# Keys, queries and values of the first image as single products, and integer additions of 512 in two-engine turns

## The chip, the cores and the metric

The kernel runs on one core of a Trainium2 chip. The metric is device time in microseconds for one execution; the time before is the median of three runs. Engines: TensorE (PE), VectorE (DVE), ScalarE (ACT), GpSimd (POOL) and SyncE (SP), which issues the DMAs.

## The reference, cut to what matters

Four images of 8 heads with 576 tokens of 64 numbers. Attention has two branches which are added: one over means of four neighbouring tokens (144), repeated four times; one over tokens nearer than four. Its output is x, 2304 rows of 512. Two layers of 512 to 2048 to 512 follow, each with a gate and with float64 weights.

```
q_d = q.reshape(B, H, Sd, 4, D).mean(axis=3)   # k_d, v_d the same
out = repeat(sm_attn(q_d, k_d, v_d), 4) + local_attn(q, k, v)   # |i - j| < 4
h = x @ w_in;  g = h * (1 / (1 + exp(-h)));  x = g @ w_out
h = x @ w2_in; g = h * (1 / (1 + exp(-1.702 * h))); out = g @ w2_out
```

## The kernel before

**Stages.** Attention goes by half images m (0 to 7) of 288 tokens; within one, by four pairs of heads. One pair of one half is a unit u = 4 m + pair (0 to 31). A finished half is scaled and split into two f16 parts (`split`: maximum over all, `rm`, `am`, `pw`; the parts `xh`, `xl`) and runs through layer 1 as 288 columns (`h1.m.p`, line 706, then `o1`, lines 823 and 851), three products per weight tile. Layer 2 takes the rows in nine tiles of 256 (`h2`, line 885; `o2`, line 964). The maximum of a layer 2 tile is spread over partitions by a diagonal (`dx`, lines 766 and 768) and a product of 128 columns (`rm`, line 775).

**Image 0 (units 0 to 7).** k and q arrive with tokens in partitions. `KT` (lines 1132 and 1134) turns k by six transposes of 96 columns and sums four tokens at a time by six f32 products of 24 columns against `four`; `KC` copies both out on ACT. `QT` (1177, 1179) and `QC` do it for q with three and three. From image 1 on DVE turns and sums instead (`KX`, `KD`, `QX`, `QD`). v is loaded twice: `vw` in windows for the local branch and `vraw` (`lv`) for the sums over four tokens, which POOL adds (`KV`, lines 1153 and 1154).

**A unit.** `SC` scores (1203, 1209), `DM`, `LC`, `LS`, `LE`, `LU`, `RC` and `LN` the two softmaxes, `DE` the exponentials of the first branch, `DN` its scaling (line 1256 on ACT, 1258 on DVE), `TP`/`TC` and `PT` turn the probabilities, `AV` (1285, 1291) multiplies by v, `UC` and `XA` add the branches, `XM` takes the maximum. `KT` uses one two-bank tile; `QT`, `TP`, `AV` and `rm` share a ring of two one-bank PSUM tiles, `pa1`.

**First weights.** Each 1 MB piece of float64 words becomes f32 integers by `ca`, `cz` (ACT), `cs` (DVE, line 332), `sg` (the sign: ACT line 345, or DVE line 337) and `cp`, an addition of 1024 integers per partition (line 349; on DVE or POOL). PE sums the upper halves (`sps`, lines 561 and 576) for a scale (`si`, `so`), and `hi` (ACT) and `lo` (DVE, line 381) make the f16 parts. `cp` of the second weights is an addition of 512 on POOL. There are eight pieces for `in` and eight for `out`, named by column block and row pair (0.0, 0.2, 1.0 ...).

**Order.** Every step is added to a plan with its engine, the tiles it reads and writes and the rings it takes. `ON` (line 25) puts chosen steps on an engine other than the usual one. `PLACES` (line 46) holds two characters per step: its place in one total order; `placed` sorts by it and refuses an order that breaks a dependency. Each engine, and SP's queue of DMAs, then works through its steps in that order; an instruction that waits holds all behind it. The list `first` (line 1478) chains the first loads softly.

## Time and profile before

| | |
|---|---|
| median of 3 runs | 893.99 us (892.43 to 894.34) |
| the profiled execution | 892.67 us, its span 890.9 us |
| PE busy | 864.1 us (97%), 10212 matmuls |
| PE weight loads | 721.5 us |
| DVE busy | 608.9 us, 1334 instructions |
| ACT busy | 470.4 us, 841 |
| POOL busy | 160.8 us, 187 |
| HBM read, written | 62.39 MB, 13.11 MB |

Busy time is the union of an engine's instructions, and matmuls are pipelined: a run of matmuls counts from the first start to the last end. An average over the span hides stages, so the rows below go by stretches of time. Matmuls of f32 are two instructions each; a transpose is one.

### The profile page before, as it was taken

To read this page: it belongs to the slowest core of one execution; us is meant where nothing else is said; L and a number is where in the kernel's file an instruction comes from. 1 tells how busy PE (TensorE), PEld (TensorE's weight loads), DVE (VectorE), ACT (ScalarE), POOL (GpSimd) and SP (SyncE) were. 2 spreads that over 40 slices of the span, in tenths; PEclk is the share of its full clock that TensorE was granted. 3 is DMA by queue.
4 is the path that set the end of the run, shared out by engine and by line. 5 is a ranking of instruction groups with operands and counts; after the bars stand their busy time and mean duration, and the time that the engine had idled before them with its cause. 6 is when DMAs were issued, how large, how long until landed. Compare 5 with 4: busy or idle time off the path is not lost.

```text
span 890.9 us, 23880 instructions
## 1 busy us (share of the span) xinstructions
PE 864.1 (97%) x10212; PEld 721.5 (81%) x10212; DVE 608.9 (68%) x1334; ACT 470.4 (53%) x841; POOL 160.8 (18%) x187
## 2 busy tenths in 40 slices
...
GB/s 241 228 244 226 199 100 86 45 120 67 120 114 117 88 156 140 152 80 135 116 61 248 101 43 1 25 1 24 2 13 1 25 24 1 37 1 25 1 25 24
DMA packets 116190, 77.04 MB, mean 86 GB/s; under 512 B 94836, under 2 KB 101492, under 8 KB 115060
## 3 DMA queue, kind: packets, MB, share of 16 engines
...
q14 instruction: 26, 0.21, 0.1%
HBM read 62.39 MB, written 13.11 MB: 85 GB/s over the span
## 4 chain that ended last, share of the span: by engine, by line
PE 84%; DVE 11%; ACT 2%; issue 1%; DMA 0%; SPq 0%; DVEq 0%; ACTq 0%
PE ops L823 19%; PE hps L706 18%; PE hps L885 18%; PE oy L964 10%; PE oz L964 5%; PE ox L964 3%; PE ul L1291 2%; PE sl L1209 2%; PE ops L851 2%; DVE g L913 1%; PE sl L1203 1%; PE ul L1285 1%; DVE wout L381 1%; PE tps L1268 1%; PE kps L1134 1%
## 5 line engine op out<-in xcount | busy, mean ns | idle before, releaser
L706 PE MATMUL hps<-xhl,win 128*128 128x288 f16 x1536 | 197.9, 287 | 0.1
L885 PE MATMUL hps<-xhl,win 128*128 128x256 f16 x1728 | 190.4, 273 | 1.3 <-DVE tg L900 1.3
L885 PEld LDWEIGHTS <-win 128*128 128x128 f16 x1728 | 169.1, 98 | 21.2 <-issue 1.6
L706 PEld LDWEIGHTS <-win 128*128 128x128 f16 x1536 | 148.5, 98 | 37.8 <-issue 0.4
L823 PE MATMUL ops<-g,wout 128*128 128x288 f16 x1344 | 171.7, 286 | 0.0
L964 PEld LDWEIGHTS <-g 128*128 128x128 f16 x1512 | 147.7, 98 | 18.6 <-issue 0.8
L823 PEld LDWEIGHTS <-wout 128*128 128x128 f16 x1344 | 129.5, 98 | 32.7 <-issue 0.6
L897 ACT ACTIVATE tg<-hps,blk 128x512 f32<-128x512 f32 x72 | 49.5, 687 | 123.9 <-PE hps L885 111.2
L900 DVE SCALAR_TENSOR_TENSOR tg<-tg,hps 128x512 f32<-128x512 f32 x72 | 49.1, 682 | 53.1 <-ACT tg L897 53.1
L913 DVE SCALAR_TENSOR_TENSOR g<-tg,g 128x896 f16<-128x896 f32 x72 | 78.1, 1097 | 0.6 <-ACT g L910 0.3
L904 POOL TENSOR_TENSOR tg<-tg 128x128 f32<-128x128 f32 x19 | 15.1, 793 | 341.9 <-DVE tg L900 341.9
L910 ACT ACTIVATE g<-tg 128x896 f16<-128x896 f32 x72 | 67.5, 945 | 16.1 <-DVE tg L906 12.0
L964 PE MATMUL oy<-wout,g 128*128 128x256 f16 x648 | 75.1, 272 | 0.0
L349 POOL TENSOR_TENSOR cs<-cs,cz 128x512 int32<-128x512 int32 x32 | 43.9, 1378 | 149.0 <-DVE cs L332 67.7
L718 ACT ACTIVATE tg<-hps,blk 128x576 f32<-128x576 f32 x64 | 47.0, 734 | 34.4 <-PE hps L706 27.7
L721 DVE SCALAR_TENSOR_TENSOR tg<-tg,hps 128x576 f32<-128x576 f32 x64 | 47.6, 744 | 18.8 <-ACT tg L718 18.8
L942 ACT ACTIVATE o<-oy,blk 128x256 f32<-128x256 f32 x27 | 12.7, 472 | 76.8 <-PE oy L964 76.8
L731 DVE SCALAR_TENSOR_TENSOR g<-tg,gs,g 128x576 f16<-128x576 f32 x56 | 46.4, 839 | 9.7 <-ACT g L728 9.7
L728 ACT ACTIVATE g<-tg,gs 128x576 f16<-128x576 f32 x56 | 42.7, 769 | 14.6 <-DVE tg L721 14.6
L948 DVE SCALAR_TENSOR_TENSOR o<-oy,blk,o 128x256 f32<-128x256 f32 x9 | 4.4, 484 | 55.4 <-PE oy L964 55.4
L324 ACT ACTIVATE st<-st 128x512 f32<-128x512 f32 (+1 forms) x48 | 39.5, 827 | 2.0 <-DMA st<-in_moe_w_out_dram 2.0
L1239 ACT ACTIVATE pd<-sl,nm 72x144 f32<-72x144 f32 x64 | 23.4, 369 | 16.3 <-DVE nm L1219 12.0
...
## 6 DMA issues: line engine op xcount, KB each, us to landing
...
```

What stands on the lines that cost most here:

```text
L349: eng.tensor_tensor(out=s, in0=s, in1=zget(), op=ALU.add)
L706: nc.tensor.matmul(o, T[w][:, kc, a, fc * P:(fc + 1) * P], T[xk][:, kc, b, :T_], start=(n == 0), stop=(n == 3 * KC - 1))
L718: ACT.activation(out=T[tg], in_=T[ps][:, :, :T_], func=AF.Tanh, scale=T["a" + bk][:, c:c + 1])
L721: DVE.scalar_tensor_tensor(out=T[tg], in0=T[tg], scalar=1.0, in1=T[ps][:, :, :T_], op0=ALU.add, op1=ALU.mult)
L731: DVE.scalar_tensor_tensor(out=T[g][:, 1], in0=T[tg], scalar=gs, in1=T[g][:, 0], op0=ALU.mult, op1=ALU.subtract)
L823: nc.tensor.matmul(o, w[:, j, a, dc * P:(dc + 1) * P], g[:, b, j % 2, :], start=(n == 0), stop=(n == 3 * NF - 1))
L885: nc.tensor.matmul(o, T[w][:, kc, a, fc * P:(fc + 1) * P], T[xk][:, kc, b, :], start=(n == 0), stop=(n == 3 * KC - 1))
L897: ACT.activation(out=four(), in_=T[ps][:, 0, :], func=AF.Tanh, scale=T["a" + bk][:, c:c + 1])
L900: DVE.scalar_tensor_tensor(out=four(), in0=four(), scalar=1.0, in1=T[ps][:, 0, :], op0=ALU.add, op1=ALU.mult)
L910: ACT.activation(out=T[g][:, 0], in_=T[tg], func=AF.Copy, scale=GS2)
L913: DVE.scalar_tensor_tensor(out=T[g][:, 1], in0=T[tg], scalar=GS2, in1=T[g][:, 0], op0=ALU.mult, op1=ALU.subtract)
L964: nc.tensor.matmul(T[bank[acc]], g[:, a, slot, :], w, start=first and p == p0 and i == 0, stop=prod in (2, 3, 4) and p == NF // 2 - 1 and ...
```

## The change

In image 0 the transposes and sums of k and q become one product per 128 columns of input: the moving matrix is `four` beside the identity (24 + 96 = 120 columns), so `KT` has six products and `QT` three, and `KC`, `QC` and the scores' addresses follow the new layout. `lv` and `KV` go for image 0; `VP` sums v by six products per pair of heads from `vw` against a new constant `vsum`, and `VC` copies the result out on ACT. `VP` takes a turn in `pa1`. `cap` makes the new constants. Each `cp` of the first weights is two additions of 512, `a` and `b`, placed one by one. In layer 2 the step `dx` goes, and `rm` has 4 columns. `GS2`, a power of two in layer 2's g, is changed. `ON` and `PLACES` are new: among other things the load of the first piece of weights is issued ahead of q and k, in the order weights 0.0, q0, k of pair 0, q1, k of pair 1, `vw` of pair 0, weights 1.0. On PE, `QT0` comes ahead of `KT0.0`, `QT1` ahead of `SC0`, and `VP0.0` stands between `KT0.1` and `SC1`. On POOL, three halves of `cp` stand ahead of `LS3`, and one between `LS3` and `LN3`. In all 26 halves go to POOL and 6 to DVE, of seven whole ones on POOL and nine on DVE before. Of `gs2`, 14 steps stay on POOL, of 19.

```diff
--- before.py
+++ after.py
@@ -20,18 +20,20 @@
 NEG = -1.0e9
 SCD = 1.0 / 128.0
 
-GS1, GS2 = 2.0 ** -15, 2.0 ** -26
+GS1, GS2 = 2.0 ** -15, 2.0 ** -19
 BAND = 4
 ON = {
-    "DVE": ("sg1.in.0.2 sg1.in.1.0 sg1.in.1.2 sg1.in.2.2 sg1.in.3.0 sg1.in.3.2 sg1.out.0.2 LS0 LN1 LN2 LS3 LS8 LN8 LN10 "
...
-    "POOL": ("cp1.out.0.0 cp1.out.0.2 cp1.out.1.0 cp1.out.1.2 cp1.out.2.0 cp1.out.2.2 cp1.out.3.2"),
-    "ACT": ("DN0 DN1 DN2 DN3 DN5 DN6 DN7 DN8 DN9 DN10 DN11 DN12 DN13 DN14 DN15 DN16 DN17 DN18 DN19 DN20 DN21 DN23 DN24 DN25 "
...
+    "DVE": ("sg1.in.0.0 sg1.in.1.0 sg1.in.2.2 sg1.in.3.0 sg1.out.0.0 sg1.out.1.0 LS0 LN0 LN2 LS4 LN5 LN8 LS9 LS10 LN10 LS13 "
...
+    "POOL": ("cp1.in.0.0a cp1.in.0.2b cp1.in.1.0a cp1.in.1.0b cp1.in.1.2b cp1.in.2.0a cp1.in.2.2a cp1.in.2.2b cp1.in.3.0a "
+             "cp1.in.3.0b cp1.in.3.2a cp1.in.3.2b cp1.out.0.0a cp1.out.0.0b cp1.out.0.2a cp1.out.1.0a cp1.out.1.0b "
+             "cp1.out.1.2a cp1.out.1.2b cp1.out.2.0a cp1.out.2.2a cp1.out.2.2b cp1.out.3.0a cp1.out.3.0b cp1.out.3.2a "
+             "cp1.out.3.2b"),
+    "ACT": ("DN2 DN4 DN5 DN6 DN7 DN8 DN11 DN12 DN13 DN15 DN17 DN20 DN21 DN22 DN30 DN31"),
...
@@ -344,9 +346,9 @@
             else:
                 ACT.activation(out=l1, in_=hi.bitcast(F32), func=AF.Copy)
 
-        def cp(eng):
-            s = r().bitcast(I32)
-            eng.tensor_tensor(out=s, in0=s, in1=zget(), op=ALU.add)
+        def cp(eng, o=slice(0, n * 512)):
+            s = r().bitcast(I32)[:, o]
+            eng.tensor_tensor(out=s, in0=s, in1=zget()[:, o], op=ALU.add)
 
...
@@ -580,9 +582,10 @@
...
-        by = on("cp" + nm, "DVE")
-        add("cp" + nm, by, 0.15 + N * 0.00235 if by == "POOL" else 0.16 + N * 0.00104, lambda: cp(POOL if by == "POOL" else DVE),
-            r=[z], w=[rkey], lock=by == "DVE")
+        for i, x in enumerate("ab"):
+            by, o = on("cp" + nm + x, "DVE"), slice(i * 512, i * 512 + 512)
+            add("cp" + nm + x, by, 0.15 + 512 * 0.00235 if by == "POOL" else 0.16 + 512 * 0.00104,
+                lambda by=by, o=o: cp(POOL if by == "POOL" else DVE, o), r=[z], w=[rkey], lock=by == "DVE")
...
@@ -761,22 +764,13 @@
...
-        def z():
-
-            DVE.tensor_reduce(out=small(L, n, 7), in_=mget(), axis=AX.X, op=ALU.max)
-            T["dg" + bk] = pools["dgx"].tile([P, P], F32, tag="dgx", name="dgx")
-            DVE.tensor_scalar(out=T["dg" + bk], in0=T["ident"], scalar1=small(L, n, 7), scalar2=None, op0=ALU.mult)
-
         def a():
             T["rm" + bk] = bank1("rm") if L.n == 1 else pools["pr"].tile([P, 512], F32, tag="pr", name="rm")
-            if L.n == 1:
-                nc.tensor.matmul(T["rm" + bk][:, :KC], ones32, mget(), start=True, stop=True)
-            else:
-                nc.tensor.matmul(T["rm" + bk][:, :P], ones32, T["dg" + bk], start=True, stop=True)
+            nc.tensor.matmul(T["rm" + bk][:, :KC], ones32, mget(), start=True, stop=True)
 
         def b():
             T["am" + bk] = small(L, n, 8)
-            DVE.tensor_reduce(out=T["am" + bk], in_=T["rm" + bk][:, :KC if L.n == 1 else P], axis=AX.X, op=ALU.max)
+            DVE.tensor_reduce(out=T["am" + bk], in_=T["rm" + bk][:, :KC], axis=AX.X, op=ALU.max)
...
@@ -791,11 +785,8 @@
...
-        if L.n == 2:
-            add("dx" + bk, "DVE", 0.45, z, r=mkey + sc2, w=["dg" + bk], alloc=[("dgx", "dg" + bk)])
-            mkey = ["dg" + bk]
...
-        add("am" + bk, "DVE", 0.16 if L.n == 1 else 0.28, b, r=["rm" + bk], w=["am" + bk])
+        add("am" + bk, "DVE", 0.16, b, r=["rm" + bk], w=["am" + bk])
...
@@ -1023,12 +1014,19 @@
...
-        T["four"] = ac.tile([P, 2, QB], F32, name="four")
+        T["vsum"] = ac.tile([P, 3, PD], F32, name="vsum")
+        POOL.memset(T["vsum"], 0.0)
+        T["four"] = ac.tile([P, TT + 2 * QB], F32, name="four")
 
     def init_cap():
         cap = T["cap"]
-        DVE.tensor_reduce(out=T["four"][:, 0], in_=T["ident"][:, :TT].rearrange("p (t r) -> p t r", r=BAND), axis=AX.X, op=ALU.add)
-        DVE.tensor_scalar(out=T["four"][:, 1], in0=T["four"][:, 0], scalar1=SCD, scalar2=None, op0=ALU.mult)
+        for e in range(3):
+            DVE.tensor_reduce(out=T["vsum"][:, e, QB * e:QB * (e + 1)].rearrange("p (i t) -> p i t", i=4),
+                              in_=T["ident"].rearrange("p (i j) -> p i j", i=4)[:, :, BAND:BAND + QB].rearrange("p i (t r) -> p i t r", r=BAND),
+                              axis=AX.X, op=ALU.add)
+        DVE.tensor_copy(out=T["four"][:, QB:QB + TT], in_=T["ident"][:, :TT])
+        DVE.tensor_reduce(out=T["four"][:, :QB], in_=T["ident"][:, :TT].rearrange("p (t r) -> p t r", r=BAND), axis=AX.X, op=ALU.add)
+        DVE.tensor_scalar(out=T["four"][:, QB + TT:], in0=T["four"][:, :QB], scalar1=SCD, scalar2=None, op0=ALU.mult)
...
@@ -1066,7 +1064,8 @@
...
-        add("lv" + nm, "SP", 0.36, lv, w=["vraw" + nm], alloc=[("vraw", "vraw" + nm)], mb=0.33)
+        if b:
+            add("lv" + nm, "SP", 0.36, lv, w=["vraw" + nm], alloc=[("vraw", "vraw" + nm)], mb=0.33)
...
@@ -1129,14 +1128,14 @@
             T[kps] = bank2("kps")
             kr = T["kraw" + nm][:TT].rearrange("p (c h d) -> p c (h d)", h=2, d=D)
             for c in range(2 * NBL):
-                nc.tensor.transpose(T[kps][:, c // NBL, (c % NBL) * TT:(c % NBL + 1) * TT], kr[:, c], T["ident"][:TT, :TT])
-            for c in range(2 * NBL):
-                nc.tensor.matmul(T[kps][:, c // NBL, HALF + (c % NBL) * QB:HALF + (c % NBL + 1) * QB], kr[:, c], T["four"][:TT, 0], start=True, stop=True)
+                nc.tensor.matmul(T[kps][:, c // NBL, (c % NBL) * (QB + TT):(c % NBL + 1) * (QB + TT)], kr[:, c], T["four"][:TT, :QB + TT],
+                                 start=True, stop=True)
 
         def cpy():
-            ACT.copy(out=T["kTs"][hp][:, BAND:BAND + S].rearrange("p (c t) -> p c t", c=2), in_=T[kps][:, :, :HALF])
+            kp = T[kps][:, :, :NBL * (QB + TT)].rearrange("p c (e t) -> p c e t", e=NBL)
+            ACT.copy(out=T["kTs"][hp][:, BAND:BAND + S].rearrange("p (c e t) -> p c e t", c=2, e=NBL), in_=kp[:, :, :, QB:])
             T[kd] = pools["at"].tile([P, 2 * PD], F32, tag="kd", name="kd", bufs=NHP)
-            ACT.copy(out=T[kd].rearrange("p (c t) -> p c t", c=2), in_=T[kps][:, :, HALF:HALF + PD])
+            ACT.copy(out=T[kd].rearrange("p (c e t) -> p c e t", c=2, e=NBL), in_=kp[:, :, :, :QB])
 
...
@@ -1160,7 +1159,25 @@
...
-        add("KV" + nm, "POOL", 2.1, sv, r=["vraw" + nm], w=[vd], alloc=[("vd", vd)])
+        vps = "vps" + nm
+
+        def vsum():
+            T[vps] = bank1("vps")
+            o = T[vps][:PD, :4 * D].rearrange("p (h c d) -> p c h d", h=2, c=2)
+            vw = T["vw" + nm].rearrange("p (h c e) d -> p c e h d", h=2, c=2)
+            for c in range(2):
+                for e in range(3):
+                    nc.tensor.matmul(o[:, c], T["vsum"][:, e], vw[:, c, e], start=e == 0, stop=e == 2)
+
+        def vcp():
+            T[vd] = pools["at"].tile([PD, 4, D], F32, tag="vd", name="vd", bufs=NHP)
+            ACT.copy(out=T[vd].rearrange("p j d -> p (j d)"), in_=T[vps][:PD, :4 * D])
+
+        if b:
+            add("KV" + nm, "POOL", 2.1, sv, r=["vraw" + nm], w=[vd], alloc=[("vd", vd)])
+        else:
+            add("VP" + nm, "PE", 1.3, vsum, r=["vw" + nm, "cap"], w=[vps], alloc=[("pa1", vps, hp + 0.45)])
+            add("VC" + nm, "ACT", act(4 * D), vcp, r=[vps], w=[vd], alloc=[("vd", vd)])
...
@@ -1173,10 +1190,9 @@
 
         def qtr():
             T[qps] = bank1("qps")
+            o = T[qps][:, :HALF + PD].rearrange("p (i c t) -> p c i t", i=5, c=NBL)
             for c in range(NBL):
-                nc.tensor.transpose(T[qps][:, c * TT:(c + 1) * TT], T[f"qraw{u}"][:TT, c * 2 * D:(c + 1) * 2 * D], T["ident"][:TT, :TT])
-            for c in range(NBL):
-                nc.tensor.matmul(T[qps][:, HALF + c * QB:HALF + (c + 1) * QB], T[f"qraw{u}"][:TT, c * 2 * D:(c + 1) * 2 * D], T["four"][:TT, 1], start=True, stop=True)
+                nc.tensor.matmul(o[:, c], T[f"qraw{u}"][:TT, c * 2 * D:(c + 1) * 2 * D], T["four"][:TT, QB:], start=True, stop=True)
 
...
@@ -1204,9 +1220,10 @@
             for bl in range(NBL):
                 for i in range(4):
                     k0 = QB * (4 * (half * NBL + bl) + i)
+                    q0 = QB * (4 * bl + i) if blocked(m) else QB * (NBL * i + bl)
                     for hh in range(2):
                         r = slice(D * hh, D * hh + D)
-                        nc.tensor.matmul(T[sl][32 * i:32 * i + 32, hh, bl * 32:bl * 32 + 32], T[qT][r, QB * (4 * bl + i):QB * (4 * bl + i) + 32],
+                        nc.tensor.matmul(T[sl][32 * i:32 * i + 32, hh, bl * 32:bl * 32 + 32], T[qT][r, q0:q0 + 32],
...
@@ -1477,7 +1493,7 @@
     by = {s.name: s for s in plan.steps}
     first = []
     for hp, p in zip(range(NHP), ("0.0", "0.2", "1.0", "1.2")):
-        first += [f"lk0.{hp}", f"lqqraw{hp}", f"vw0.{hp}", f"lv0.{hp}", "ldst1in." + p]
+        first += [f"lk0.{hp}", f"lqqraw{hp}", f"vw0.{hp}", "ldst1in." + p]
     first += ["ldst1in." + p for p in ("2.0", "2.2", "3.0", "3.2")]
     for c in range(NC):
         first += [f"ldst1out.{c}.0", f"lqqraw{NHP + c}", f"ldst1out.{c}.2"]
```

## Rows read from the trace of the kernel before

**Rows 1.** Busy time by stretches: PE, PEld, DVE, ACT, POOL; clock, DMA share, GB/s.
```profile
0.00:20.00 20.00, 12.27 (x108) 11.66 (x110) 4.46 (x15) 7.31 (x16) 6.79 (x29) 1.00 0.99 252
20.00:64.00 44.00, 36.92 (x588) 31.93 (x587) 38.74 (x88) 36.60 (x66) 7.57 (x8) 1.00 1.02 241
64.00:143.00 79.00, 72.20 (x1144) 55.45 (x1142) 75.13 (x180) 63.93 (x109) 30.55 (x23) 0.98 0.66 159
143.00:510.00 367.00, 366.86 (x4970) 289.04 (x4969) 256.08 (x631) 210.53 (x451) 75.94 (x70) 1.00 0.43 115
510.00:550.00 40.00, 38.74 (x335) 32.57 (x334) 38.90 (x47) 24.10 (x27) 5.21 (x8) 1.00 0.09 33
550.00:891.00 341.00, 337.12 (x3078) 300.81 (x3075) 195.56 (x376) 127.96 (x176) 34.76 (x50) 1.00 0.04 15
```

**Rows 2.** Waits of PE to 64 us: total, times, longest.
```profile
PE kps L1132 <- DMA kraw<-in_k_dram: 6.1, 1, 6.1
```

**Rows 3.** Waits of PE from 64 to 145 us.
```profile
PE tps L1268 <- ACT pd L1256: 2.4, 1, 2.4
```

**Rows 4.** Waits of DVE ending from 13 to 22 us.
```profile
DVE sc L1224 <- PE sl L1209: 13.3, 2, 9.3
DVE smr L1250 <- ACT pd L1239: 1.1, 1, 1.1
```

**Rows 5.** Timeline of PE, single pieces: start us, us, line, tiles, shape, count.
```profile
40.53 1.22 PE L1132 MATMUL kps<-ident,kraw 96*128 96x96 f32 x6
41.55 2.65 PE L1134 MATMUL kps<-four,kraw 96*128 96x24 f32 x12
44.02 0.72 PE L1177 MATMUL qps<-ident,qraw 96*128 96x96 f32 x3
44.53 1.37 PE L1179 MATMUL qps<-four,qraw 96*128 96x24 f32 x6
...
63.76 3.08 PE L706 MATMUL hps<-xhl,win 128*128 128x288 f16 x12
...
68.37 1.63 PE L706 MATMUL hps<-xhl,win 128*128 128x288 f16 x12
...
98.98 0.39 PE L773 MATMUL rm<-blk,ones 128*128 128x4 f32 x2
...
552.78 0.39 PE L775 MATMUL rm<-dgx,ones 128*128 128x128 f32 x2
```

**Rows 6.** Timeline, single pieces of DVE and POOL near 106 and 127 us.
```profile
105.86 2.38 POOL L349 TENSOR_TENSOR x<-x,z 128x1024 int32<-128x1024 int32 x1 [4.71 <-PE spo L576]
105.92 2.35 DVE L1250 TENSOR_SCALAR smr<-smr 128x8 f32<-128x8 f32 x1
...
127.13 2.13 DVE L460 TENSOR_TENSOR prod<-wsm,ibin 128x1 f32<-128x1 f32 x1
```

**Rows 7.** Groups by line and form: count, busy us, mean ns, idle before.
```profile
L349 POOL TENSOR_TENSOR cs<-cs,cz 128x512 int32<-128x512 int32 x32 | 43.9, 1378 | 149.0 <-DVE cs L332 67.7 <-DVE cz L337 30.5 <-ACT g L728 18.4
...
L1153 POOL TENSOR_TENSOR vraw<-vraw 72x512 f32<-72x512 f32 x16 | 22.1, 1381 | 28.1 <-DMA vraw<-in_v_dram 28.1
...
L349 POOL TENSOR_TENSOR x<-x,z 128x1024 int32<-128x1024 int32 x7 | 16.5, 2374 | 8.1 <-PE spo L576 4.7 <-ACT z L345 3.4
...
L345 ACT ACTIVATE z<-st 128x1024 f16<-128x1024 f32 x9 | 12.3, 1363 | 0.1
...
L349 DVE CUSTOM_DVE_ANT_0 x<-x,z 128x2048 uint16<-128x2048 uint16 x9 | 10.9, 1212 | 0.2
L332 DVE TENSOR_SCALAR x<-st 128x1024 int32<-128x1024 int32 x16 | 10.9, 681 | 1.9 <-ACT st L324 1.9
...
L1261 DVE TENSOR_TENSOR sc<-sc,smr 128x192 f32<-128x192 f32 x15 | 5.7, 382 | 0.1
L337 DVE TENSOR_SCALAR z<-st 128x1024 uint16<-128x1024 uint16 x7 | 5.5, 788 | 0.5 <-ACT z L328 0.3
...
L1258 DVE TENSOR_TENSOR pd<-pd,smr 72x288 f32<-72x288 f32 x5 | 2.8, 568 | 0.0
```

More of the change, by code (lines that the diff above doesn't have):

```diff
@@ new lines @@
+    "3k2S3p3u1Q2y2C2O2U2W3R3X171c1e1l1O221F1P1T20252c2u2w2P2Y3x3I353a3Z4l44662m323h3c4q3L3S4w4L2K3o3H4h4r4u4H4X5Q3w4n5b4R5o5d5l5t5I3B4O505c"
+    "5R5K5O616e4C5G5Z5Y64696i6v7f4z5s6a5C6C6r6I6K6Y5r6W6P7a7g7j7z7p7x65797L7i7R7n7r7W824J536f6q6z6F6b6o6H6U70766S747m7C7A7J7O7S7Y8586889u0d"
+    "0i0t0O0b0c0j0o0m0v0p0r0y0z0C0A0D0M0I0R0Z12140l0u1j1p0g0s0x0E0G0P13161a1d1g1f1h1m1k1t1D1H1J191i1Y29151b1n1w1x1G1A1E1M1N281X242b2a2e2k2p"
+    "2D1K232s2I1U21272j2f2v2l2t2z2A2E2B2F2H2J2M2T2V2X303334393g3b363f3C5a737e8w1W2q374t313e3i3n3q3r3s3v3y3A3E3D3J3W4042484b4D383j3z3M3G3Q3N"
@@ new lines @@
+    "3U41454K4f4o4y4M4Q4V4Z514e4m4p4B4v4E4G4N4W565f585g5j5q5v5B5E5M5254595i5e5m5k5p5w5A5F5D5J5L5P5S5X6062686n6D7I7P8Gci3l3t6h4k3d4i6J55678x"
+    "7G6x4F8Q7N5V3Y46495n5y636j6g6p6k6G6O6Q6T757b7k6Z7K7U839z3P3T8n5T6c6t726M7E8a8d8f8h8k8l8o8r8u8B8H8L9w7v7Z8K7o7u898j8p8t8C8J8O8P8T8V9197"
+    "9b9f9k9m9o8A8I9g8m8s8R928X958Z93989a9d9c9p9v9h9A9G9J9K9Pa1a7a9aqa8cd7t908U9H8E9i9L9R9T9V9Wa4aaacaeafaraxanaBaHaJb79E9Ua2adavataDaGaKaM"
+    "aNaOaSaVaUb8bcbfbhayaPaTaZb0b3b9bgbkblbnbobsbzbqbLbUbZcxapb6bpbwbGbCbKbMbVbWc0bYc7cbc5cfckcmcBcGcJcTd3dxdde99q9ncvaA8DbQbdbmbFdochcpdr"
@@ new lines @@
+    "egd7dibDcgbabybBcrcucwczcAcFcKcLcMcWdgdkcOdydBdDfibNbSd1cncqcDcId4dmd8dadqdsdPdFdMejekeoeyeBeDc6ccdEcQd0dHdUdTe0e5ereueweAexeIeLeSeVf1"
+    "f3f5e4e6eCdGdKeFeJeOeReQeUeWeXfaeYf6f9fcfffkfmfrfHfNfQfZgdi6mvd2enfhf4ebeMfpfufvfyfxfEfLfMg3fPfVg2g8gngqgtjOf0fzfDg1fKgefUfYghgjgogmgz"
+    "gCgIgQgYh0h4fCgugygAgDgKgGgJgNgPh1gVhci0hMi5iaidiefRfTh6h9hWhghZi1i3i7ibi9ikinihiuiAiEjAk3k7k9kgknktnvcafqhFfFe7gXiJgkg9hRlkgHjyjSkcma"
+    "j4g6gOgrgEiBiLiNj0iPj3jbjdjfjujBjKjVjzkfkikpkrhqjhhfhajajqjQjtjTjxjGjWjXk0k1kBkMk6kYl4l5mCj5j8iKiYkukxkEkFkIkJkXkZl1lQlolwlPlWmimomqmr"
```

71 lines of the change are left out of this document (29 added, 42 removed), and 11 rows, old and new, of the table ON.

## The prediction

> **What bounds the kernel now.** I read the busy table by stretches first, then what each engine waited for, then single pieces of the timeline. In the stretches [rows 1] the reader is to see three regimes. From 143 us on TensorE (PE) has no time to give: 366.86 of 367 us are busy to 510, 38.74 of 40 to 550, 337.12 of 341 to the end. Only less matmul work could shorten that part. From 64 to 143 us PE is busy 72.20 of 79 us while VectorE (DVE) is busy 75.13: here DVE is the last one, and PE loses 6.8 us. From 20 to 64 us DVE (38.74 of 44), PE (36.92) and ScalarE (ACT, 36.60) are all near full. Before 20 us everything waits for the first scores. PE's first instruction waits 6.1 us for k's transfer [rows 2], DVE waits twice, 9.3 and 4.0 us, for PE's first two scores [rows 4]. One single wait of PE after 64 us is long, 2.4 us for a normalised probability [rows 3].
>
> The granted clock stands as 1.00 in each of the first two stretches, but the pieces say otherwise: the first twelve matmuls of the first product (128x288) take 3.08 us and the next twelve 1.63 us [rows 5]. So PE runs at its level of 1.2 GHz to about 66.8 us and at 2.4 GHz after; what it did just before the rise was a back-to-back run of sums and of that product. All attention work of the first half image therefore has half the clock.
>
> The time can thus change in two ways: by when the first product starts (63.76 us) and by how much PE loses until 143 us.
>
> **The change part by part.**
>
> *q's and k's products.* Per pair of heads of image 0, six transposes (1.22 us) and six sums of two passes each (2.65 us) become six products of two passes. The start of the sums shows their pitch, 2.65 us for 12, about 0.21 us, whose weights are 128 columns wide and whose data are only 24. Whether 120 columns fit under the same pitch: at full clock a pair with 4 columns and a pair with 128 columns both take 0.39 us [rows 5], so yes. The other end: 120 columns take 0.2 us at half clock (the transposes' 96 columns have a pitch of 0.16), and behind the weights that adds 2.4 us per k. I take hidden: −1.0 us per k (4 times), −0.5 per q at half clock (q's transposes 0.72 of which 0.2 is tail; units 0 to 5), −0.25 for two later ones. −7.0 us of PE before the first product.
>
> *v's sums on PE.* In image 0 four loads of v (288 KB each) and four pairs of GpSimd (POOL) additions (the first 1.38 us [rows 7]) go; 4 x 6 products of 128 columns in two passes come. A pair of that size is 0.22 us apart at full clock (0.39 with its end [rows 5]), so six are 1.3, and 2.6 at half clock: +10.4 us there, +5.2 if the clock were up; below that only if 72 weight columns were quicker, which the 128 columns of data forbid. Four ACT copies of 256 elements come too, each under a third of the 1024-element one (1.36 [rows 7]); ACT loses two DN steps in exchange. v's sums also take a turn in the ring of two one-bank PSUM tiles, so that the transposes of the probabilities (TP), queued behind them on PE, wait for that ACT copy too: under 0.5 us, four times, part of rival C. In sum PE gets +3.4 us before the first product. It has 7 us to spare there from 20 to 64, so part is hidden: between 0 and +3.4, I take +1.7.
>
> *Additions of 512.* DVE gives up nine additions of 1.212 us and gets six halves. A half is between 0.61 (half) and 0.8 us; at 0.69 it is 4.1 instead of 10.9: −6.8. POOL gets 26 halves of about 1.27 us (its own 512 form; a mean of 1378 with waits) instead of 7 of 2.37 us [rows 7]: 33 instead of 17 us, in 143 us where it is busy 45 [rows 1], so there is room. The sign copies: DVE has six instead of seven (−0.8), ACT one more (1.36). DN of units 0 to 10: DVE does five instead of one, +2.3; LS and LN nine instead of seven, +0.8 [rows 7]. Sum on DVE −4.5. The three more sums in the start-up step "cap" lie in DVE's first wait of 9.3 us: nothing; products of q and k wait for "cap", but it ends before k lands.
>
> *The two engines' port.* DVE's tiny L1250 took 2.35 us beside a POOL addition of 2.38, another 2.13 [rows 6]; alone each is under 0.2. These two cost 4.1 us for 7 additions. A hold half as long is met half as often and costs half: 0.6 x (1.27/2.37)² = 0.17 for each of 26, 4.4 in all, +0.2. Ends: none at all (−4.1), and half of each held (26 x 0.63 − 4.1 = +12.3). The Trainium skill (GPSIMD Engine Reference, Specifications) says that GpSimd shares its SBUF interfaces with VectorE and contends with DVE instructions in a two-port mode or with two SBUF inputs; the 2.35 us agrees. By that rule the new halves collide with the many DVE steps of these kinds, which is a rival below.
>
> *Order.* The first weights' load (1 MB) now goes out ahead of q, k, and the first v load is gone. SP's queue is in order, so k lands later: 1.2 MB more less 0.3 MB at the 252 GB/s of [rows 1] is up to 3.5 us. In return q's products and two of k's are shorter and start with q; the first scores start between 0.5 us earlier and 3 us later. While DVE waits 4.0 and 1.1 us after the first scores [rows 4], it now has a sign copy (0.79), a DN (0.57), an LN (0.38) and a shift (0.68): 2.4 us out of the full stretch. Between 0 and −2.4 for both together; I take −1.2. The other queue moves (POOL's LS3 and LN3 behind three and one halves) cost at most one half each and are inside the port's bound.
>
> *Second layer.* The maximum over partitions loses two DVE instructions per tile, and its product shrinks from 128 to 4 columns at equal 0.39 us [rows 5]. DVE has 145 us to spare after 550 us, so this gives nothing; the five gs2 steps that go from POOL to DVE cost nothing either. Between 510 and 550 DVE is full (38.90 of 40 [rows 1]) and PE loses 1.3 us: ±1. The factor GS2 costs nothing.
>
> *Sum.* −4.5 (DVE) −1.2 (hole) +0.2 (port) +1.7 (PE) = −3.8 us. The profiled execution took 892.67 us (span 890.9), the median of three is 893.99, 1.3 more. 892.67 − 3.8 + 1.3 = 890.2 us.
>
> **The rivals.**
>
> *A: the clock rises early.* The first 64 us become products back to back (k, then v: over 5 us in one run) where transposes and thin sums stood. If PE reaches 2.4 GHz well before 63 us, v's products cost no 1.7, the first product takes 1.63 instead of 3.08 (−1.45), and DVE's hole fills wholly (−1.2): −3.8 − 4.4 = −8.2, 885.8 us. For it: the denser run. Against it: 5.4 us without a gap from 40.53 us on [rows 5] left the level at 1.2 GHz. The Trainium skill (TensorE: Matmul & The Clock Gate, PE-mode transpose) says that full clock does not engage for transposes; here they go. The 40.53 us run agrees, and by that rule this rival gains.
>
> *B: the port (slower).* Place: DVE from 20 to 143 us, where it is full. If each of the 26 halves holds DVE for 0.5 us on average, the port costs 13 − 4.1 = +8.9 instead of +0.2: −3.8 + 8.7 = +4.9, 898.9 us. It decides the sign from 0.31 us per half on (4.0 + 4.1 over 26). For it: 2.35 and 2.13. Against: five of the seven before held nothing long.
>
> *C: PE at half clock is last.* The whole +3.4 lands in front of the first product and the hole is not filled: −4.5 + 0.2 + 3.4 = −0.9, 893.1 us. For it: PE 36.92 of 44 us busy.
>
> **How the numbers follow.** Forecast 0.42, A 0.20, B 0.20, C 0.18. A difference under 0.2% (1.8 us) cannot be told from none. Faster: 0.38 of the forecast's, A whole, a little of C: 0.61; slower: nearly all of B, 0.19; 0.20 between. The forecast's own range is 887.5 to 892.5 (hole and PE's cost at either end); 885 to 898.5 leaves out a part of A and half of B.
>
> **What would show it.** Right: the first 128x288 product starts 2 to 4 us before 63.76, PE is full from about 139 us on, DVE's nine long additions are six of about 0.69 us, k's group is a single run of 2.6 us. A is seen by v's products at 1.3 us and twelve first matmuls at 1.63; B by several DVE instructions of a microsecond beside POOL's halves; C by PE without a gap before the first product. The forecast is wrong if PE loses time after 143 us, which the new order of all later steps could cause and no row here prices.

## The result and the profile after

The changed kernel takes 883.31 us (median of 4 runs, 882.96 to 885.88) against 894.16 of before beside it: ratio 0.9895, with a 95% interval of [0.9871, 0.992]. A second series gave 883.26 against 893.59, 0.9879 [0.9863, 0.9894]. That is 10.3 to 10.9 us faster; the forecast was 3.8 us (890.2, in a range from 885 to 898.5), and the measured time lies below that range.

The profiled executions hide part of this. The one of before (892.67) is among its fastest, both of after (885.88 and 885.37) are its slowest, so the traces differ by 6.8 us. Start of the first product of each stage in the timelines of PE (us; a_dx, described below, has the changed kernel's instructions up to layer 2):

| | before | after | after, again | a_dx |
|---|---|---|---|---|
| first 128x288 product | 63.76 | 61.41 | 61.19 | 58.53 |
| second half image's | 143.86 | 137.04 | 136.74 | 134.04 |
| layer 2's | 528.93 | 523.97 | 523.45 | 522.32 |
| end of the span | 890.9 | 884.1 | 883.6 | (889.0) |

From before to after: -2.35 us up to the first product, -4.5 up to the second half, +1.9 up to layer 2 (steps of the second half that had been done before 143 us now come later), -1.8 in layer 2.

After, busy time by stretches (columns as in [rows 1]):
```profile
0.00:20.00 20.00, 13.12 (x117) 11.72 (x125) 5.38 (x22) 8.65 (x16) 2.55 (x25) 1.00 1.06 257
20.00:64.00 44.00, 36.73 (x605) 32.18 (x606) 35.62 (x91) 38.92 (x69) 17.03 (x15) 0.70 0.78 219
64.00:143.00 79.00, 73.30 (x1218) 57.24 (x1217) 76.75 (x182) 61.90 (x107) 36.00 (x32) 0.99 0.68 159
143.00:510.00 367.00, 366.45 (x4922) 288.30 (x4920) 262.31 (x638) 207.89 (x435) 70.98 (x71) 1.00 0.44 118
510.00:550.00 40.00, 40.00 (x357) 34.56 (x355) 39.11 (x52) 23.64 (x28) 5.94 (x9) 1.00 0.00 1
550.00:884.00 334.00, 330.16 (x3013) 294.10 (x3011) 187.56 (x362) 124.43 (x172) 20.32 (x33) 1.00 0.04 15
```
The first line is 0 to 20 us, the second 20 to 64, and so on. From 20 to 64 us DVE went from 38.74 to 35.62 us busy and ACT from 36.60 to 38.92: ACT is now the fullest. POOL more than doubled. The DMA share fell from 1.02 to 0.78: the second loads of v are gone. PE's loss between 510 and 550 us is gone.

Groups of after by line and form (count, busy us, mean ns, idle before), answering to [rows 7]:
```profile
L351 POOL TENSOR_TENSOR x<-x,z 128x512 int32<-128x512 int32 x26 | 37.4, 1453 | 49.3 <-DVE x L334 28.4 <-DVE z L339 11.5 <-ACT z L347 9.3
...
L334 DVE TENSOR_SCALAR x<-st 128x1024 int32<-128x1024 int32 x16 | 12.5, 788 | 0.6 <-ACT st L326 0.6
...
L1278 DVE TENSOR_TENSOR sc<-sc,smr 128x192 f32<-128x192 f32 x14 | 8.0, 568 | 0.2
...
L351 DVE CUSTOM_DVE_ANT_0 x<-x,z 128x1024 uint16<-128x1024 uint16 x6 | 4.6, 761 | 0.0
```
DVE's additions fell from 10.9 to 4.6 us. Other DVE steps of unchanged form became longer: `cs` from 681 to 788 ns (16 of them, 1.7 us), `LN` from 382 to 568. The longest of them lie beside POOL's work: a `cs` of 1.79 us at 94 us and an `LN` of 2.10 at 219.

Timeline of PE in after, single pieces (columns as in [rows 5]):
```profile
8.33 2.88 PE L1131 MATMUL kps<-four,kraw 96*128 96x120 f32 x12
...
42.02 2.73 PE L1170 MATMUL vps<-vw,vsum 128*72 128x128 f32 x12
...
48.60 1.53 PE L1170 MATMUL vps<-vw,vsum 128*72 128x128 f32 x12 [0.21 <-DVE xf L1322]
...
61.41 3.06 PE L709 MATMUL hps<-xhl,win 128*128 128x288 f16 x12
```
k's group is one run of 2.88 us where 1.22 + 2.65 stood. v's group takes 2.73 us at 1.2 GHz and 1.53 at 2.4. In windows of 4 us the granted clock is 0.50 from 28 to 32 us, 0.72 from 36, 0.50 from 40, 0.93 from 44, 1.00 from 48 and 0.50 from 56 to 64: the level rose more than once, and by the first product it had fallen again.

Windows of 5 us from 105 to 115 us, where before has its longest wait of PE after 64 us (before, then after; columns as in [rows 1]):
```profile
105.00:110.00 5.00, 2.30 (x67) 1.59 (x65) 4.89 (x12) 3.32 (x6) 2.38 (x1) 1.00 1.02 173
110.00:115.00 5.00, 4.43 (x23) 2.99 (x23) 4.86 (x16) 5.00 (x8) 0.51 (x1) 0.66 0.65 119
```
```profile
105.00:110.00 5.00, 4.10 (x34) 3.13 (x32) 4.88 (x10) 4.95 (x7) 3.34 (x2) 1.00 0.35 79
110.00:115.00 5.00, 4.09 (x36) 3.33 (x36) 4.90 (x15) 5.00 (x9) 0.00 (x0) 1.00 0.02 3
```
Before, PE is idle for 2.7 us while the 2.35 us hold of [rows 6] (a short DVE instruction that lasts as long as the POOL addition beside it) and the wait of [rows 3] pass, and then gets 0.66 of its clock. After, PE is busy 4.10 of the same 5 us and the clock stays at 1.00. (The longest of that DVE instruction now takes 1.25 us.) This execution is no rule: in a_dx, with the same instructions, the clock falls to 0.74 from 95 to 100 us behind a gap of 1.5.

Waits of PE in layer 2 (before, then after, 505 us to the end):
```profile
PE hps L885 <- DVE tg L900: 1.3, 2, 0.9
PE oy L964 <- DVE g L913: 0.2, 1, 0.2
```
```profile
PE oy L955 <- DVE g L904: 0.6, 1, 0.6
```

### The profile page after: what moved, and what is told of

Same layout as the page of the kernel before. It is cut to its first block, busy times and chain, and to the rows that moved or that the text cites. A ratio compares the mean times of both kernels' runs of the same rounds, so it can differ in the third digit from the quotient of the medians.

```text
span 884.1 us, 23833 instructions
## 1 busy us (share of the span) xinstructions
PE 859.8 (97%) x10212; PEld 718.1 (81%) x10212; DVE 606.7 (69%) x1342; ACT 465.4 (53%) x824; POOL 152.8 (17%) x184
## 4 chain that ended last, share of the span: by engine, by line
PE 84%; DVE 8%; ACT 4%; DMA 2%; SPq 1%; issue 1%; DVEq 0%; ACTq 0%
PE hps L876 20%; PE ops L814 19%; PE hps L709 19%; PE oy L955 10%; PE oz L955 5%; PE ox L955 2%; PE ul L1308 2%; PE sl L1226 1%; DMA kraw<-in_k_dram 1%; PE sl L1219 1%; PE ul L1302 1%; PE ops L842 1%; SPq L1051 1%; DVE wout L383 1%; DVE g L904 1%
## 5 line engine op out<-in xcount | busy, mean ns | idle before, releaser
L901 ACT ACTIVATE g<-tg 128x896 f16<-128x896 f32 x72 | 67.3, 944 | 14.5 <-DVE tg L897 10.4
L351 POOL TENSOR_TENSOR cs<-cs,cz 128x512 int32<-128x512 int32 x32 | 41.9, 1316 | 154.9 <-DVE cs L334 54.8
L895 POOL TENSOR_TENSOR tg<-tg 128x128 f32<-128x128 f32 x14 | 9.7, 691 | 293.6 <-DVE tg L891 264.1
L351 POOL TENSOR_TENSOR x<-x,z 128x512 int32<-128x512 int32 x26 | 37.4, 1453 | 49.3 <-DVE x L334 28.4
```

Of the source, the lines that this page charges most:

```text
L351: eng.tensor_tensor(out=s, in0=s, in1=zget()[:, o], op=ALU.add)
L901: ACT.activation(out=T[g][:, 0], in_=T[tg], func=AF.Copy, scale=GS2)
```

## The experiments

A name with b_ is the kernel before with an edit, one with a_ the changed kernel with an edit. Each was timed beside before, whose medians were 893.49 to 894.22 us; a result is its median, the ratio to before with its 95% interval, and the difference in us. Three theories were on record: T1, the additions of 512 (DVE's time and the port); T2, the products of 120 columns and the clock; T3, the new order.

**One edit alone in the old order.**

*b_split*: each whole addition as two of 512 in its place.
```diff
+            for i in range(n):
+                o = slice(i * 512, i * 512 + 512)
-            s = r().bitcast(I32)
-            eng.tensor_tensor(out=s, in0=s, in1=zget(), op=ALU.add)
+                s = r().bitcast(I32)[:, o]
+                eng.tensor_tensor(out=s, in0=s, in1=zget()[:, o], op=ALU.add)
```


> The kernel before with every addition of the first weights as two of 512 in a row on the same engine; nothing else. Theory 1 (port: shorter holds are what gained): 2 to 4 us faster than before, the two holds of over 2 us on VectorE gone, the 2.4 us wait of PE after 106 us gone. Theory 2 (the products of 120 columns and the clock they raise) and theory 3 (the new order and engines): no difference, -1 to +1 us.

Measured: 892.48 us, 0.999 [0.9981, 0.9998], -1.1 us. No DVE instruction up to 146 us takes over 2 us any more, but the wait of PE after 106 us is still there (2.8 us). T1 falls for the old order.

*b_merge*: `KT` and `QT` as products of 120 columns.
```diff
-                nc.tensor.transpose(T[kps][:, c // NBL, ...], kr[:, c], T["ident"][:TT, :TT])
-                nc.tensor.matmul(T[kps][:, c // NBL, ...], kr[:, c], T["four"][:TT, 0], start=True, stop=True)
+                nc.tensor.matmul(T[kps][:, c // NBL, ...], kr[:, c], T["four"][:TT, :QB + TT], start=True, stop=True)
```


> The kernel before with q's and k's transposes and sums as one product of 120 columns, in the order of before; nothing else. Theory 2: 3 to 6 us faster, the first 128x288 product starts 3 to 4 us before 63.8 us, PE at 2.4 GHz in part of the first 60 us. Theory 1 and theory 3: 0 to 1.5 us faster (PE has slack before the first product).

Measured: 891.02, 0.9972 [0.9962, 0.9981], -2.6 us: less than T2's 3 to 6, more than the 0 to 1.5 of the others. The first 128x288 product starts at 60.76 us, 3.0 earlier, and takes 3.02 us, as at 1.2 GHz: the gain comes without a higher clock there.

*b_dx*: no diagonal in layer 2.
```diff
-            DVE.tensor_reduce(out=small(L, n, 7), in_=mget(), axis=AX.X, op=ALU.max)
-            DVE.tensor_scalar(out=T["dg" + bk], in0=T["ident"], scalar1=small(L, n, 7), ...)
-                nc.tensor.matmul(T["rm" + bk][:, :P], ones32, T["dg" + bk], start=True, stop=True)
+            nc.tensor.matmul(T["rm" + bk][:, :KC], ones32, mget(), start=True, stop=True)
```


> The kernel before, in its own order, with the diagonal of layer 2 gone (two VectorE instructions per tile, the product of 128 columns is one of 4). If the diagonal is what the stage of layer 2 lost: from layer 2's first product to the end 360.1 to 360.5 us instead of 361.97, the time 892. If the waits of TensorE between 510 and 550 us are the order's: 361.4 to 361.8, the time 893.1 to 893.5.

Measured: 892.79, 0.9993 [0.9982, 1.0005], no difference. Layer 2 takes 361.5 us (before 361.97, after 360.1), and the waits stand as before:
```profile
PE hps L879 <- DVE tg L894: 1.3, 2, 0.9
```
So some 0.45 of layer 2's 1.8 us can be the diagonal's; 1.3 are these two waits, which only the new order removes.

**One edit undone in the new order.**

*a_whole*: whole additions again, 10 on POOL and 6 on DVE.
```diff
-                lambda by=by, o=o: cp(POOL if by == "POOL" else DVE, o), ...
+                (lambda by=by, o=o: cp(POOL if by == "POOL" else DVE, slice(0, 1024))) if i == at else (lambda: None), ...
```


> The changed kernel with the first weights' additions whole again (1024): ten pieces on GpSimd, six on VectorE, in the changed order. Theory 1: 3 to 6 us slower than the changed kernel (886 to 889). Theory 2 and 3: 0 to 2 us slower (VectorE has 3.1 us more work: six times 1.21 instead of 0.69).

Measured: 889.84, 0.9968 [0.9956, 0.998], 6.5 us above the changed kernel. Its groups:
```profile
L351 POOL TENSOR_TENSOR x<-x,z 128x1024 int32<-128x1024 int32 x10 | 25.9, 2586 | 28.3 <-ACT z L347 12.2 <-DVE z L339 8.1 <-PE spo L578 8.0
...
L351 DVE CUSTOM_DVE_ANT_0 x<-x,z 128x2048 uint16<-128x2048 uint16 x6 | 7.9, 1319 | 0.0
```
and its stretch from 95 to 105 us, in which the clock falls as in before:
```profile
95.00:100.00 5.00, 1.76 (x54) 1.33 (x55) 4.97 (x9) 4.26 (x5) 1.47 (x1) 0.68 1.05 276
100.00:105.00 5.00, 5.00 (x32) 3.73 (x33) 4.08 (x13) 0.82 (x4) 0.51 (x1) 0.64 0.84 108
```
DVE's additions take 3.3 us more, one of POOL's takes 2586 ns where a half took 1453, and PE is idle for 3.2 of 5 us before the clock is at 0.64. T1 holds in this order.

*a_transp*: transposes and sums apart (b_merge's edit, reversed).


> The changed kernel with q's and k's transposes and sums separate again. Theory 2: 4 to 6 us slower than the changed kernel (887 to 889): 7 us more on PE at half clock ahead of the first product. Theory 1 and 3: 0 to 2 us slower.

Measured: 889.22, 0.9955 [0.9942, 0.9968], 5.9 us above the changed kernel, as T2 said; the first 128x288 product at 64.35 us.

*a_vpool*: v of image 0 loaded a second time and summed on POOL (in the place of `VC`), PE's `VP` empty.
```diff
+            if b == 0:
+                T[f"vraw{b}.{hp}"] = pools["ld"].tile([PD, 4, BAND * D], F32, tag="vraw", name="vraw", bufs=1)
+                nc.sync.dma_start(out=T[f"vraw{b}.{hp}"], in_=v[b, 2 * hp:2 * hp + 2].rearrange(...))
-            add("VP" + nm, "PE", 1.3, vsum, ...)
-            add("VC" + nm, "ACT", act(4 * D), vcp, ...)
+            add("VP" + nm, "PE", 1.3, lambda: None, ...)
+            add("VC" + nm, "ACT", act(4 * D), sv, ...)
```


> The changed kernel with v of image 0 summed as before: loaded a second time, added on GpSimd, copied there; no products of v on TensorE. T2 (v's products cost TensorE 12 to 14 us of busy time ahead of 64 us and 10 of it at half clock, but buy the dense run): without them the first 128x288 product starts at 59 to 61 us, and the time is 0 to 2 us below the changed kernel's, 881.5 to 883.5; if they are what brings the clock up at 44 us, the products of the first half stay at half clock, +1 to +2, 884.5 to 885.5. T1 (GpSimd is the engine that has no room to give): 4 pairs of additions of 1.38 us in front of the integer additions delay these, DVE's scaled parts come later, +3 to +6, 886.5 to 889.5. T3 (the order decides, and it was made for v on TensorE): over +2 as well, with TensorE idle growing between 20 and 143 us.

Measured: 890.61, 0.9966 [0.9953, 0.9978], 7.3 us above the changed kernel: beyond T1's +3 to +6, and as T3 said, with PE's idle time from 20 to 64 us at 17.3 instead of 7.3 us. Waits to 66 us (total, times, longest) of ACT, and of SP's queue to 70, and the stretch from 20 to 64:
```profile
ACT st L326 <- DMA st<-in_moe_w_in_dram: 7.3, 5, 3.6
ACT z L330 <- DMA st<-in_moe_w_in_dram: 4.1, 1, 4.1
...
SPq L1092 <- POOL vd L1156: 7.6, 2, 4.0
```
```profile
20.00:64.00 44.00, 26.70 (x453) 23.56 (x454) 35.09 (x82) 33.79 (x55) 22.12 (x19) 0.65 1.04 241
```
In after only the second of ACT's waits is there. PE has 10 us less to do in the stretch and is late all the same (first 128x288 product at 66.03 us): ACT waits 7.3 us for weights, and what is queued behind on it waits too. Two causes are on record. The DMA share is back at 1.04. And the second v has one buffer (`vraw`, `bufs=1`): SP, with `vw` and the weights queued behind, is held 7.6 us until POOL has summed the pair before. They are not separated. (The loads stand ahead of `vw` here; another place, or a second buffer, was not tried.)

*a_dx*: the diagonal again, its two DVE instructions directly ahead of the product.


> The changed kernel with layer 2's maximum spread by the diagonal again (two DVE instructions and a product of 128 columns per tile). If the removed pair is what shortened the part from the first product of layer 2 to the end (before 361.97, after 360.1 us): +1.5 to +2 us, 885, with the stage back at 361.5 to 362. If that gain is the order around 510 to 550 us: the stage stays at 360.1 to 360.5 and the time within 0.5 of the changed kernel's.

Measured: 891.16, 0.9973 [0.9964, 0.9982], 7.9 us above the changed kernel, 6.6 of them in layer 2 (366.7 us against 360.1). There
```profile
PE rm L775 <- DVE dgx L774: 5.7, 5, 1.5
```
stands: PE waits for the pair. In before they stood earlier in DVE's order and PE waited for none. So most of the price is that of the place, not of the instructions.

**Order without edits, edits without order.**

*a_order*: all four undone in the new order (the four edits above). 

> The changed kernel's order and engines with its four edits undone: whole additions, transposes and sums apart, v on GpSimd, the diagonal. T3 (the order holds most of the gain by itself): 885 to 890. T1 and T2 additive (the halves and the products each worth some 6 us in this order, v and the diagonal 0 to 3): 883.3 + 6.5 + 5.9 + 0 to 3 = 895.5 to 898.5, slower than the kernel before. If the two overlap (either alone removes what the other would): 889 to 892.

Measured: 905.96, 1.0145 [1.0124, 1.0165], 12.3 us slower than before, over every range on record. T3 in the form "the order holds the gain by itself" falls. But 5.0 of the 12.3 us are layer 2 (366.9 us against 361.97), where the diagonal stands in a_dx's bad place, and v is loaded as in a_vpool.

*b_three* (b_split, b_merge and b_dx together) and *b_four* (also v on PE, `VP` behind `KT0.1` and `TP1`, ahead of `TP2` and `TP3`):


> As the one before this, with v left on GpSimd: additions of 512, products of 120 columns, no diagonal, in the order of the kernel before. If the edits add up in the old order: 893.6 - 1.1 - 2.6 - 0 to 1.5 for the diagonal = 888.4 to 889.9. If the two of the front hide one another: 890.5 to 891.

> The kernel before, in its own order and with its own engines, with all four edits: the additions of 512 (two in place of each whole one, one after the other), the products of 120 columns, v of image 0 summed on TensorE (each copy behind or ahead of the copy of the probabilities of its pair; no second load of v), no diagonal in layer 2. What is left to the changed kernel is the order and the choice of engines. T1 and T2 (the edits carry the gain): 884 to 886. T3 (edits and order pay only together; the single edits gave 1.1 and 2.6 here): 888 to 890, and the rest up to 883.3 is the order's.

Measured: b_three 888.81, 0.9947 [0.9927, 0.9966], -4.8 us: the single edits add up. b_four 899.15, 1.0056 [1.0044, 1.0069], 5.6 us slower than before, where both theories had it faster. v's sums cost 10.3 us there. Waits of PE in b_four to 72 us, and of SP to 60:
```profile
PE vps L1169 <- DMA vw<-in_v_dram: 4.5, 1, 4.5
...
PE vps L1169 <- DVE x L351: 3.7, 1, 3.7
...
SPq L524 <- DVE z L337: 8.4, 1, 8.4
```
The old queue brings `vw` late, and `VP`, with all that is queued behind it on PE, waits. The second wait is put down to a DVE step on the weights, from which `VP` reads nothing; the `vw` of that pair was issued only at 28.0 us, after SP had stood 8.4 us for a buffer of weights, and `VP` started at 35.5.

**The clock and the early load.**

*a_warm*: twelve products of 512 columns into q's tile while PE waits for q. *a_keep*: 13 of 512 or 384 columns in three later waits. *a_both*: both. Their results are not used.
```diff
+            for _ in range(12 if u == 0 else 0):
+                nc.tensor.matmul(T[qps][:, :512], ones, T["warm"], start=True, stop=True)
...
+            for _ in range(5 if u == 3 else 0):
+                nc.tensor.matmul(T[tps][:, :512], ones, T["warm"], start=True, stop=True)
...
+            for _ in range(3 if u == 3 else 0):
+                nc.tensor.matmul(lo[2][:, :512], ones, T["warm"], start=True, stop=True)
...
+                for _ in range(5 if (c, j) == (3, 0) else 0):
+                    nc.tensor.matmul(T[ps][:, 1, P:], ones, T["warm"][:, P:], start=True, stop=True)
```


> The changed kernel with twelve added products of 512 columns (bf16, ones) that go into q's own tile before q's first products, in the time in which TensorE waits for q; their result is written over. T2 (half clock until 64 us is a cost): if TensorE then reaches 2.4 GHz before 20 us and keeps it, VP and the products of k go at half their time, the first product starts 1 to 3 us earlier and takes 1.53 instead of 3.06 us: 880 to 882.5. If the clock falls back in the waits up to 20 us, nothing: 883 to 884. If the clock ahead of 64 us is hidden by DVE: the level changes in the pieces and the time does not.

> The changed kernel with 13 added bf16 products (ones, 512 or 384 columns, nothing used) in three waits of TensorE: five ahead of the transposes of the probabilities of pair 3 (a wait of 1.54 us), three ahead of its products with v (0.82), five ahead of the sums of weights 3.0 (1.13). If the level at 1.2 GHz from 56 to 65 us follows from these waits and TensorE is last there: the sums of 3.2, the products of q 4 and q 5 and the first 128x288 products go at 2.4 GHz in every execution, the first of them starts at 58 to 59 us (61.2 in the two profiles of the changed kernel), and the time is 881 to 882. If VectorE or ScalarE is last there: the level rises and the time stays at 883.3. If the added products come in the way of the real ones: 884 to 885.

> As the one before this, and also twelve such products ahead of q's first ones, in the first wait of TensorE. If both hold: 880 to 881.5. If the early ones only lengthen the wait behind the first scores: as the one before this.

Measured: a_warm 882.40, 0.9874 [0.9855, 0.9892]; a_keep 883.82, 0.9891 [0.9873, 0.9908]; a_both 882.32, 0.9873 [0.9856, 0.989]. None can be told from the changed kernel's 0.9879 [0.9863, 0.9894]. In a_keep the level is held:
```profile
53.98 1.89 PE L1199 MATMUL qps<-four,qraw 96*128 96x120 f32 x12
57.32 0.47 PE L1223 MATMUL sl<-kd,qT 64*72 64x144 f32 x4 [1.46 <-ACT qT L1203]
...
58.28 1.66 PE L711 MATMUL hps<-xhl,win 128*128 128x288 f16 x12
```
q's two groups take 1.89 us (2.90 in after) and the first product 1.66, and between them PE waits 1.46 us for ACT's copy of q, where after has no wait: what the clock gives up to the first product, ACT takes. The profiled execution is 881.54 us, the other four 883.49 to 885.64.

*a_tkeep*: a_keep's products in a_transp. 

> The changed kernel with transposes and sums of q and k apart again, which took 889.22 us, and the 13 added products in TensorE's three waits ahead of the first 128x288 product. In the profile without them the last of q's and the first 128x288 products ran at 1.2 GHz to about 68 us. If the 5.9 us that the separate products cost are mostly that level: the first 128x288 product in 1.6 instead of 3.06 us, its start 2 to 4 us earlier, 885 to 886.5. If they are TensorE's and ScalarE's longer work between 8 and 45 us: 888 to 889.5.

Measured: 889.27, 0.9946 [0.9927, 0.9964]; a_transp had 889.22. q's transposes run at 2.4 GHz, and PE then waits for ACT's copy:
```profile
61.08 0.44 PE L1198 MATMUL qps<-ident,qraw 96*128 96x96 f32 x3
...
64.43 0.76 PE L1224 MATMUL sl<-kd,qT 64*72 64x144 f32 x4 [1.31 <-ACT qT L1204]
```
The first 128x288 product starts at 65.81 us and still takes 2.53 us, so the level was held only in part of this stretch. That the time did not move speaks against the level as the main part of the 5.9 us; it does not settle it.

*a_load2*: the first weights behind q's and k's first loads.
```diff
+    move("ldst1in.0.0", "lqqraw1")
+    for x in ("cz1.in.0.0", "ca1.in.0.0"):
+        move(x, "sg1.in.0.0")
```


> The changed kernel with the first weights loaded behind q's and k's first loads, and cz and ca of 0.0 ahead of VectorE's sign step of 0.0 in the one order, which puts them behind the copies of q and k on ScalarE. If the delay of q and k by the 1 MB ahead of them is a cost: the first scores 2 to 3 us earlier and 881 to 882.5. If VectorE needs the early piece to fill its wait: 884.5 to 886.5. In between, no difference.

Measured: 883.16, 0.988 [0.9863, 0.9897]: no difference, though the first scores start at 10.97 us instead of 12.43. (A form with the two moved steps ahead of `LE0`, and so behind `sg1.in.0.0`, which then took an older content, had 884.76; its time shows nothing.) *a_lkeep* adds a_keep's products: 

> Both mild variants together: the first weights behind q's and k's first loads, and the 13 added products. If their profiles (first 128x288 product at 57.4 and 58.3 us) stand for typical executions and add up: 880 to 881.5. If the variants only shift which execution is profiled: 882.5 to 884, as the changed kernel.

Measured: 883.36, 0.9892 [0.9873, 0.9912]. No version beats the changed kernel measurably.

*after_again*: 

> The changed kernel once more, beside these runs. Its first profiled execution, 885.88 us, lay 2.6 above the median of its four runs, so its trace shows too little of the gain. Expected: a median of 883 to 884, and a profile within 1 us of it, in which the first 128x288 product starts at 58.5 to 59.5 us (61.41 in the first profile) and the second half image's at 134 to 135 (137.04). If the early gain is not there in a typical execution either: 61.4 and 137, and the missing 2.6 us stand behind 143 us.

Measured as told at the top. The profiled execution (885.37 us) is again the longest of its runs and has its first product at 61.19 us, so the early start on record did not show in it; it showed in a_dx.

**Where the edits act.** Single executions, us:

| | first 128x288 product | from there to the second half image's | layer 2 to the end |
|---|---|---|---|
| before | 63.76 | 80.10 | 361.97 |
| b_split | 63.76 | 80.07 | 361.96 |
| b_merge | 60.76 | 79.62 | 362.0 |
| b_three | 61.11 | 79.15 | 361.4 |
| b_four | 71.38 | 79.15 | 361.2 |
| after | 61.41 | 75.63 | 360.1 |
| a_whole | 60.77 | 80.98 | 360.2 |
| a_transp | 64.35 | 75.76 | 360.1 |
| a_vpool | 66.03 | 75.75 | 360.5 |

The additions of 512 pay between the two products, and only in the new order: whole ones make that part 5.4 us longer there (a_whole), halves in the old order leave it as it was (b_split). The products of q, k and v act almost wholly ahead of the first product.

## Why the prediction was wrong

The direction was right, the size was not: -10.3 to -10.9 where -3.8 was forecast.

**The step that failed is the sum of the two terms ahead of the first 128x288 product**: PE's, "between 0 and +3.4, I take +1.7", which is v's +10.4 less the 7.0 of q and k, and the order's, "Between 0 and −2.4 for both together; I take −1.2". They were priced one by one and added, +0.5 for both. In the runs v's sums and the new order are worth something only together. With the other three edits in, v on PE costs 10.3 us in the old order (b_four against b_three), the new order with v on POOL costs 1.8 (a_vpool against b_three, with v's loads where a_vpool has them), and the two together give 5.5 (883.31 against 888.81). The forecast missed by 6.5 to 7.1 us, and most of that lies here.

PE's work and clock up to its first 128x288 product (b_three, b_four, after; columns as in [rows 1]):
```profile
0.00:61.11 61.11, 43.74 (x651) 37.26 (x651) 42.98 (x110) 43.43 (x81) 14.41 (x37) 1.00 1.01 258
```
```profile
0.00:71.38 71.38, 47.73 (x698) 42.02 (x699) 42.50 (x113) 44.29 (x85) 6.23 (x30) 0.78 0.81 208
```
```profile
0.00:61.41 61.41, 47.26 (x698) 42.25 (x699) 38.91 (x108) 45.26 (x78) 17.57 (x38) 0.81 0.87 235
```
Of the 10.3 us in the old order, 4.0 are PE's longer work and 6.3 are idle time of PE; that the sum is near the priced 10.4 is chance. The new order does the same work with 9.5 us less idle time (14.15 against 23.65). The forecast counted what PE and ACT get. It named the four loads and POOL's additions that go, but priced only the first load's 0.3 MB, in k's arrival. Taking the products back in the new order costs 7.3 us (a_vpool): the four loads return to a queue whose DMA share is 1.0 to 64 us [rows 1], SP is held for the one buffer, and ACT waits 7.3 us more for weights.

**Behind it stands the way of summing.** The edits were priced by rows of the old order, and there such prices hold: the three without v add up to -4.8 (b_three). In the new order undoing the additions costs 6.5, the transposes 5.9, v 7.3, the misplaced diagonal 7.9, together 27.6, and all at once 22.7 (905.96 - 883.31). Order alone is +12.3 (5.0 of them the diagonal's place), edits alone +5.6, both together -10.3: with the edits in, the order is worth 15.8 us (899.15 against 883.31).

*Additions.* Six halves took 4.6 us (forecast 4.1), and the whole ones 10.9. This term was sound: with the port's +0.2 it says -4.3, and the part in which the additions act became 4.5 us shorter. What it left out is the fall of the clock behind PE's idle time, which costs the products behind it some 1.8 us in before: the first 48 products of `o1`, whose pieces of PE's timeline are (before, then after)
```profile
110.57 7.71 PE L851 MATMUL ops<-g,wout 128*128 128x288 f16 x48 [0.87 <-DVE tg L721]
```
```profile
103.06 3.10 PE L709 MATMUL hps<-xhl,win 128*128 128x288 f16 x24 [0.39 <-DVE tg L724]
106.00 3.10 PE L842 MATMUL ops<-g,wout 128*128 128x288 f16 x24
```
take 7.71 us, where 24 of that shape are 2.94 apart at full clock, 5.9 for 48. The fall is missing in both profiles of after and there in a_whole. It is there in a_dx too, whose part up to the second half image (75.51 us) is no longer than after's 75.63, so what the fall costs the whole is not shown. Splitting in place doesn't remove it: b_split has PE idle for 2.8 of the same 5 us and then a clock of 0.50.

*Port.* Summed over the DVE instructions to 146 us that took over 0.25 us longer than the shortest of their form, the excess is 7.0 us before and 8.0 after (a_whole: 11.3): +1.0 where +0.2 was forecast (0.17 for each of 26, less 4.1, is +0.3) and +8.9 by rival B, which is out.

*q's and k's products.* 120 columns do fit under the pitch of 0.21 us (12 in 2.88 with the end). Undoing this costs 5.9 us in the new order and the edit gives 2.6 in the old.

*Rival A.* The level does rise before the first product, and by how much differs between executions: the granted clock of 20 to 64 us is 0.70 in after and 0.81 in a_dx, with the first product 2.9 us apart (3.06 us long in after, 2.39 in a_dx). The products of k and v of the second pair, in after and then in a_dx, show where:
```profile
27.41 2.77 PE L1131 MATMUL kps<-four,kraw 96*128 96x120 f32 x12
...
30.45 2.77 PE L1170 MATMUL vps<-vw,vsum 128*72 128x128 f32 x12
```
```profile
26.39 1.50 PE L1137 MATMUL kps<-four,kraw 96*128 96x120 f32 x12
...
28.76 1.48 PE L1176 MATMUL vps<-vw,vsum 128*72 128x128 f32 x12
```
The distance of the two executions is 0.6 us at 26 us and 3.0 when these groups are done. By layer 2 it is 1.65. Raising the level with added products (a_warm, a_keep, a_both) gained nothing that can be measured. How much of the gain is the clock's in a typical execution stays open: only profiled ones have a timeline. In a_tkeep three transposes of 96 columns took 0.44 us against 0.72 [rows 5], behind products that had raised the level. The Trainium skill (TensorE: Matmul & The Clock Gate, Part 4: PE-mode transpose) says that full clock does not engage for transposes; here they run at it once it is up.

*The early load and the hole.* The first scores start at 12.43 us, against 12.07 before, and DVE's waits up to 22 us add up to 11.7 us, against 14.4: the hole is 2.7 us smaller. a_load2 shows no difference in time, so what the place of the early load gains or costs in the whole is not measurable.

*Layer 2* was priced at "±1" and gave -1.8: two waits of 1.3 us in all are gone with the new order. Ahead of it the +1.9 of steps that now come later stand against this, and no term had them.

Not separated: how the -4.5 us from the first product to the second half image's divide between DVE's shorter work, the clock's fall and steps put off.
